# Numerators and seven-product sums accumulated in PSUM, the division on VectorE, and one more chunk in seven products

## The chip, the cores and the metric

The kernel runs on one core of a Trainium2 chip. A core has a matrix engine (TensorE, "PE" in the profile; its weight loads are "PEld"), three engines for elementwise work (VectorE "DVE", ScalarE "ACT", GpSimd "POOL") and a sync engine "SP", which here only issues DMAs. Each engine runs its own instructions strictly in the order of its own queue. Matmuls write into PSUM, eight banks of 2 KB per partition; DVE and ACT read and write PSUM and SBUF, in this kernel POOL touches SBUF only.

The metric is the device time of one execution in microseconds (us). Durations inside the execution come from one profiled execution.

## The reference

Two parts, one behind the other. First an attention with exponential features, for 8 batches and 8 heads, 576 positions of 64; then a feed-forward with the maximum of three projections, on 4608 tokens of 512:

```python
def phi(x):                                   # x: [8, 8, 576, 64], w_phi: [64, 128]
    proj = x @ w_phi
    proj = proj - max(abs(proj), axis=-1)
    return concat([exp(proj), exp(-proj)], axis=-1)
q_p, k_p = phi(q), phi(k)
kv  = einsum('bhsf,bhsd->bhfd', k_p, v);  z = sum(k_p, axis=2)
num = einsum('bhsf,bhfd->bhsd', q_p, kv)
den = einsum('bhsf,bhf->bhs', q_p, z)[..., None] + 1e-06
x = (num / den).transpose(0, 2, 1, 3).reshape(4608, 512)

h = maximum(maximum(x @ w1, x @ w2), x @ w3)  # w1, w2, w3: [512, 768]
out = h @ w_out                               # w_out: [768, 512]
```

## The kernel before

**Attention in 16 units.** A unit u is half a batch: four heads, that is two pairs `pr` of two heads `ab`. Per unit, PE projects keys and queries (line 545), DVE takes the maximum of the absolute values (line 549), and ACT takes the two exponentials `Ek` (line 553) and `Eq` (line 633) out of PSUM, for g = 0 and g = 1 (plus and minus). POOL multiplies the values with the exponentials of the key maxima (`vab`, line 597), PE makes the key-value matrices (`kvps`, line 616), which ACT or DVE copies to `kv_sb` (line 623).

**Numerators** (lines 674 to 743). For each of the four heads of a unit, PE makes ten products of 65 columns (64 of the numerator, 1 of the denominator): five blocks c of 128 positions for each g, into two banks `psn[0]` and `psn[1]` (line 683). DVE scales the first bank by `sq` into an SBUF tile `y` (line 692) and adds the second bank (line 695). For a pair of heads DVE then takes the reciprocal of the ten denominators (line 740) and POOL multiplies, `x_sb = y * rden` (line 741). From `x_sb` the tokens are turned into `xT`, by PE for units 0 and 1, by a DMA transpose on SP's queue for the others (line 773).

**Feed-forward in 9 chunks.** Chunk c (0 to 7) takes the first 512 positions of batch c, that is of units 2c and 2c+1; chunk 8 takes the last 64 positions of all batches. The weights are changed on the chip: w2 and w3 become w2 - w1 and w3 - w1 (six POOL subtractions, line 982), w1 @ w_out is made once (`pm`, line 1018), and h @ w_out becomes x @ (w1 @ w_out) (called straight, line 924) plus max(0, x(w2-w1), x(w3-w1)) @ w_out (called down, line 929). An ordinary chunk makes 12 groups of four 512-column matmuls (`ups`, line 891); the first six groups are relu'd out of PSUM by ACT or DVE (lines 905, 907), DVE takes the maximum with the other six (line 901).

**Chunks in seven products** (`seven_products`, lines 780 to 867; chunks 6, 7, 8). Here the two projections of a chunk are made as a 2 x 2 block product with seven products p1 to p7 in place of eight, of 256 columns (line 820), with sums of token blocks `sums` (four additions, `xs`, line 799) and sums of weight blocks `w_sums` (twelve POOL subtractions, `ws`, line 996). Every product has a bank of its own. For each of the three pairs of column blocks ACT copies p1 (line 845) and DVE makes seven additions (line 829), two of them for intermediate sums that stay in SBUF (u2, u3) and one (v) that is needed for one result; then two relus on ACT (line 862) and two maxima on DVE (line 864).

**What sets the order.** Every step is a node with a number, in the order in which the program creates it. A table written out by hand into the file (`PLAN`, read by `plan`, line 245) lists all nodes in the order in which they are emitted, with the engine that does each (T is PE, D DVE, A ACT, G POOL, S SP) and the indices of the buffers that it is the first to use, banks among them. So the table sets the order of every queue, the choice of engine where a step may go to several, and the sharing of the buffers. `fill` (line 268) puts idle matmuls between the early ones. The four weight loads are issued on POOL's queue (line 952); in the old table POOL issues w1, w_out and w2 right behind the loads of the first four units and w3 later.

## Time and profile before

| | |
|---|---|
| Time before, median of 3 runs | 276.3 us (275.75 to 281.68) |
| The profiled execution: its own time | 276.54 us |
| Its span, first to last instruction | 274.7 us |
| Mean granted clock of TensorE | 0.993 |
| PE, DVE, ACT, POOL busy | 265.6, 241.5, 214.2, 186.9 us |
| Chain of work that ended last, by engine | PE 89%, DVE 4%, ACT 3%, DMA 2% |
| `ups` of ordinary chunks, line 891 | 288 matmuls |
| `ups` of seven products, line 820 | 252 matmuls |
| DVE additions on seven products, line 829 | 63, 679 and 680 ns in the middle |
| POOL `x_sb`, line 741 | 32, 39.7 us |

A row of a group of instructions gives the line, the engine, the operation, what it writes and reads, the shapes and the count; then the busy time, the mean length of one, and the idle time ahead of it with what ended it. A row of windows gives a stretch of the span, and for each engine its busy time and the count in brackets. A row of the timeline or of the chain gives the start, the length and what ran. PE's ends are modelled: rows of neighbouring matmuls overlap, so PE's cost is read from the chain, where a group of n matmuls stands with the time that it took.

### The profile page before, as it was taken

The page shows a single profiled execution, that of the slowest core. Times are in us where ns is not written, and L with a number is a line of the kernel's source. Part 1 is how long each engine was busy: PE and PEld are TensorE (multiplying, and loading weights), DVE is VectorE, ACT ScalarE, POOL GpSimd, SP SyncE. Part 2 cuts the span into 40 slices and gives each one's busy share as a digit, 9 for nine tenths or more (in the row PEclk, how much of TensorE's full clock was granted, in tenths as well). Part 3 has the DMA queues.
Part 4 walks back from the last instruction along what each step waited for, and adds up shares of the span by engine and source line. Part 5 has one row for each costly group of instructions (what it writes and reads, how often), then busy time and mean ns, then how long its engine had stood idle before and what let it go on. Part 6 is the DMA issues. An engine that isn't in the chain of part 4 may idle for free.

```text
span 274.7 us, 8748 instructions
## 1 busy us (share of the span) xinstructions
PE 265.6 (97%) x3540; PEld 159.8 (58%) x3540; DVE 241.5 (88%) x489; ACT 214.2 (78%) x516; POOL 186.9 (68%) x183
## 2 busy tenths in 40 slices
PE   7789999999999999999999999999999999999994
PEld 4458744566565556565655455655548766686652
DVE  3799999999999888988888998999898999998871
ACT  3999999999999999779878989799987443254241
POOL 6798999999769951987569279937899856600000
PEclk9989999999999999999999999999999999999999
DMA  6999999999999999999999994596505053020253
GB/s 143 258 220 209 210 195 242 249 175 193 193 195 160 262 178 254 212 217 204 180 201 164 240 216 70 108 248 156 128 6 161 2 98 115 0 76 4 47 154 144
DMA packets 76200, 44.54 MB, mean 162 GB/s; under 512 B 52672, under 2 KB 67328, under 8 KB 76160
## 3 DMA queue, kind: packets, MB, share of 16 engines
q1 hardware_dynamic: 60880, 31.93, 53.6%
q0 software_dynamic: 14912, 11.77, 29.1%
q8 instruction: 27, 0.44, 0.6%
q10 hardware_dynamic: 368, 0.30, 0.3%
q14 instruction: 13, 0.11, 0.1%
HBM read 34.64 MB, written 9.44 MB: 160 GB/s over the span
## 4 chain that ended last, share of the span: by engine, by line
PE 89%; DVE 4%; ACT 3%; DMA 2%; issue 0%; POOLq 0%
PE ups L891 21%; PE ops L929 17%; PE ops L924 12%; PE ups L820 10%; PE psn L683 8%; PE kvps L616 7%; PE psm L642 3%; PE psq L545 3%; PE psk L545 3%; DMA qk_bf<-in_k_dram 2%; PE pm L1018 2%; ACT Eq L633 2%; DVE mk L549 2%; PE tps L508 1%; ACT Ek L553 1%; PE pst L545 1%
## 5 line engine op out<-in xcount | busy, mean ns | idle before, releaser
L633 ACT ACTIVATE Eq<-psm 128x512 bf16<-128x512 f32 (+1 forms) x160 | 81.7, 579 | 6.7 <-PE psm L642 6.1
L597 POOL TENSOR_TENSOR vab<-v_raw,em 128x1152 bf16<-128x1152 f32 (+1 forms) x36 | 68.3, 1906 | 17.5 <-ACT em L591 17.4
L553 ACT ACTIVATE Ek<-psk 128x512 bf16<-128x512 f32 x128 | 71.6, 641 | 2.2 <-DVE mk L549 1.2
L891 PE MATMUL ups<-xT,w_bf 128*128 128x512 bf16 x288 | 69.7, 380 | 0.0
L741 POOL TENSOR_TENSOR x_sb<-y,rden 128x640 bf16<-128x640 f32 x32 | 39.7, 1252 | 20.8 <-DVE rden L740 20.1
L929 PE MATMUL ops<-wout_bf,hT 128*128 128x512 bf16 (+2 forms) x222 | 52.0, 374 | 0.0
L549 DVE TENSOR_REDUCE mq<-psq 128x4 f32<-128x512 f32 x64 | 41.2, 681 | 4.8 <-PE psq L545 4.6
L549 DVE TENSOR_REDUCE mk<-psk 128x4 f32<-128x512 f32 x64 | 42.2, 681 | 2.2 <-PE psk L545 1.4
L891 PEld LDWEIGHTS <-w_bf 128*128 128x128 bf16 x288 | 25.0, 98 | 26.3 <-issue 1.3
L692 DVE TENSOR_TENSOR y<-psn,sq 128x325 f32<-128x325 f32 x64 | 30.6, 492 | 3.9 <-PE psn L683 3.1
L929 PEld LDWEIGHTS <-hT 128*128 128x128 bf16 x222 | 20.7, 98 | 21.7 <-DVE hT L864 0.5
L683 PEld LDWEIGHTS <-Eq 128*128 128x128 bf16 x640 | 26.1, 98 | 11.4 <-issue 2.3
L695 DVE TENSOR_TENSOR y<-y,psn 128x325 f32<-128x325 f32 x64 | 30.2, 487 | 2.1
L939 ACT COPY osb<-ops 128x512 f32<-128x512 f32 (+2 forms) x29 | 16.9, 582 | 17.2 <-PE ops L929 16.8
L829 DVE TENSOR_TENSOR parts<-ups,parts 128x512 f32<-128x512 f32 (+1 forms) x45 | 29.1, 679 | 1.1 <-PE ups L820 0.8
L683 PE MATMUL psn<-kv_sb,Eq 128*128 128x65 bf16 x640 | 28.7, 194 | 0.4 <-ACT Ek L553 0.4
L545 PEld LDWEIGHTS <-qkT 64*128 64x128 bf16 x576 | 18.6, 95 | 16.2 <-issue 12.3
L901 DVE TENSOR_TENSOR hT<-hT,ups 128x512 bf16<-128x512 bf16 x36 | 23.9, 676 | 2.0 <-PE ups L891 1.3
L924 PE MATMUL ops<-xT 128*128 128x512 bf16 x96 | 24.6, 381 | 0.0
L862 ACT ACTIVATE hT<-hT 128x512 bf16<-128x512 bf16 x18 | 10.8, 628 | 16.5 <-DVE hT L829 16.5
L616 PE MATMUL kvps<-vab,Ek 64*128 64x65 bf16 x1152 | 22.0, 192 | 0.0
L616 PEld LDWEIGHTS <-Ek 64*128 64x128 bf16 x1152 | 20.5, 96 | 1.0 <-issue 0.2
(84 smaller groups left out, 391.5 us busy)
## 6 DMA issues: line engine op xcount, KB each, us to landing
v_raw<-in_v_dram SPq DMA_DIRECT2D x16, 576.0 KB, 5.4
out_dram<-osb SPq DMA_DIRECT2D x31, 256.0 KB, 3.0
qk_bf<-in_k_dram POOLq DMA_DIRECT2D x15, 288.0 KB, 6.9
qk_bf<-in_q_dram POOLq DMA_DIRECT2D x15, 256.0 KB, 7.3
w_bf<-in_moe_w_dram POOLq DMA_DIRECT2D x3, 768.0 KB, 15.7
tail_raw<-in_q_dram SPq DMA_DIRECT2D x16, 64.0 KB, 4.6
out_dram<-osb SPq DMA_DIRECT2D x8, 128.0 KB, 2.3
wout_bf<-in_moe_w_out_dram POOLq DMA_DIRECT2D x1, 768.0 KB, 18.7
```

The source lines that it names most:

```text
L545: nc.tensor.matmul(ps[s]()[:, i, :], lhsT=qkT()[r, n, :], rhs=wph[r, :], start=True, stop=True)
L549: return nd(kind, {"DVE": 0.598 if n == 4 else 0.331}, lambda: nc.vector.tensor_reduce(dst(m()), ps()[:, 0:n, :], AXX, ALU.max, apply_abso ...
L553: return nd("ek", {"ACT": 0.478 if n == 4 else 0.264}, lambda: nc.scalar.activation(dst(Ek[g]()), ps()[:, 0:n, :], EXP, scale=1.0 - 2.0 * ...
L597: made.append(chosen(n_, lambda n_, g=g, t0=t0, t1=t1: (nc.vector if n_.eng == "DVE" else nc.gpsimd).tensor_tensor(vab()[:, g, t0:t1, 0:D] ...
L616: nc.tensor.matmul(kvps[ab]()[:, pr, g, :], lhsT=Ek[g]()[r, t, :], rhs=vab()[r, g, t, :], start=(pr == prs[0] and g + j == 0), stop=(pr == ...
L633: return nd("eq", {"ACT": 0.478 if n == 4 else 0.264}, lambda: nc.scalar.activation(Eq[g]()[:, t0:t0 + n, :], ps()[:, 0:n, :], EXP, scale= ...
L683: nc.tensor.matmul(psn[g]()[:, i, :], lhsT=Eq[g]()[:, t, :], rhs=kv()[:, pr, ab, g, :], start=True, stop=True)
L692: n_ = nd("xu", {"DVE": 0.064 + 0.0676 * n_t}, lambda: nc.vector.tensor_tensor(yv(y()), ps(0), sq_of(sq()).unsqueeze(len(shape) - 1).to_br ...
L741: divs[pr] = nd("x", {"POOL": 1.2}, lambda pr=pr, y=y, rden=rden: nc.gpsimd.tensor_tensor(x_sb()[:, pr].rearrange("p t a d -> p a t d"), y ...
L891: nc.tensor.matmul(ups()[:, o * n:(o + 1) * n], lhsT=w_bf[i + (not plain)][:, ct, jj * P:(jj + 1) * P], rhs=tokens_of(ct)[:, cols] if halv ...
L924: nc.tensor.matmul(ops_()[:, 0:hi - lo], lhsT=tile_of(ct, tt), rhs=line_w[c_i > MOVE][:, ct, lo:hi], start=(ct == 0), stop=False)
L929: nc.tensor.matmul(ops_()[:, 0:hi - lo], lhsT=hT()[:, j, tt * P:(tt + 1) * P], rhs=wout_bf[:, j, lo:hi], start=plain and j == 0, stop=(j = ...
```

## The change

Five things, all at once.

1. **Numerators in PSUM.** For each head, PE makes the five products of g = 0 into one bank; DVE scales that bank in place by `sq` (`xu`, PSUM to PSUM); PE then makes the five products of g = 1 onto the same bank, accumulating; DVE takes the reciprocal of five denominators out of PSUM (`xr`) and multiplies from PSUM into `x_sb` (`x`). The tile `y` and the second bank are gone. The multiplication is no longer on POOL.
2. **Seven-product sums in PSUM.** p6, p7 and p4 are accumulated onto p1's bank and p3 onto p5's. ACT or DVE copies the running sums to SBUF three times per pair (`kept`: s1, u2, u3), DVE makes three additions (c11, c22, c12), one operation that takes the maximum of the bank, zero and h (`hp`), and one maximum (`hx`) after one relu on ACT (`hr`).
3. **Chunk 5 in seven products too**, next to 6, 7 and 8.
4. **Sums of weights.** Three of the four live in an SBUF tile of their own, `w_sum`; the fourth overwrites half of w3 - w1 in place, after the last ordinary chunk has read it (chunk 4's last six groups). They no longer take buffers from the q and k loads.
5. **A new table** of 1752 nodes in place of 1687. `rden` gets eight buffers (it had three), the output tile `osb` three in place of four. Among the many moves of order: POOL issues w1 behind the first loads, w_out behind the first of the unit-0 products `vab`, and w2 and w3 only behind all `vab` products of units 0 and 1, w2 ahead of the key load of unit 4 and w3 behind it. w3's and w2's subtractions come after that, then `vab` of units 2 and 3.

```diff
-YS = 3
+YS = 8
-OSB = 4
+OSB = 3
-SEVEN = (6, 7, 8)
+SEVEN = (5, 6, 7, 8)
...
-            for pr in range(2):
-                y = buf("y", YS, [P, 2, 5, W], FP32)
-                rden = buf("rden", YS, [P, 2, 5, 1], FP32)
-                sums = [numerators(5, [(pr, ab, range(5))], lambda t, pr=pr, ab=ab: t[:, 2 * pr + ab, :],
-                                   (n_kvs[pr] + eqs[pr] + eqs["t"], [n_sq]), (y, lambda t, ab=ab: t[:, ab])) for ab in range(2)]
-                n_ = nd("xr", {"DVE": 0.122}, lambda y=y, rden=rden: nc.vector.reciprocal(rden(), y()[:, :, :, D:W]), sums, [y, rden])
-                divs[pr] = nd("x", {"POOL": 1.2}, lambda pr=pr, y=y, rden=rden: nc.gpsimd.tensor_tensor(
-                    x_sb()[:, pr].rearrange("p t a d -> p a t d"), y()[:, :, :, 0:D], rden().to_broadcast([P, 2, 5, D]), ALU.mult),
-                              [n_], [y, rden, x_sb], port=True)
+        def numerators(pr, ab, n_sq):
+            psn = bank("psn", [P, 5, W])
+            rden = buf("rden", YS, [P, 5, 1], FP32)
+
+            def nmm(g):
+                for c in range(5):
+                    t = 8 * (c % 2) + block(2 * pr + ab, c // 2) if c < 4 else NQ + pr
+                    nc.tensor.matmul(psn()[:, c, :], lhsT=Eq[g]()[:, t, :], rhs=kv()[:, pr, ab, g, :],
+                                     start=g + c == 0, stop=True,
+                                     skip_group_check=True)
+            ready = n_kvs[pr] + eqs[pr] + eqs["t"]
+            a = nd("N", {"PE": 0.157}, lambda: nmm(0), ready, [Eq[0], kv, psn])
+            n_ = nd("xu", {"DVE": 0.41}, lambda: nc.vector.tensor_tensor(
+                psn(), psn(), sq()[:, 2 * pr + ab, :].unsqueeze(2).to_broadcast([P, 5, W]), ALU.mult), [a, n_sq], [psn, sq],
+                    locks=[psn])
+            a = nd("N", {"PE": 0.157}, lambda: nmm(1), ready + [n_], [Eq[1], kv, psn])
+            n_ = nd("xr", {"DVE": 0.1}, lambda: nc.vector.reciprocal(rden(), psn()[:, :, D:W]), [a], [psn, rden], locks=[psn])
+            return nd("x", {"DVE": 0.4}, lambda: nc.vector.tensor_tensor(
+                x_sb()[:, pr, :, ab, :], psn()[:, :, 0:D], rden().to_broadcast([P, 5, D]), ALU.mult), [n_], [psn, rden, x_sb],
+                      locks=[psn])
...
-            p1 = product((0, 0), lambda: w_bf[1][:, 0:2], ready + d2, [])
-            s1 = chosen(ff("us", {"ACT": 0.482, "DVE": 0.598}, None, [p1[1]], [p1[0], one_], locks=[p1[0]]),
-                        lambda n_: copy_on[n_.eng](one()[:, 0], p1[0]()))
-            s1 = part(one, 0), one_, s1
-            p2 = product((0, 1), lambda: w_bf[1][:, 2:4], ready + d2, [])
-            own += [h(0), h(1)]
-            c11 = joined(p2, s1, own[0], hT)
-            p6 = product(1, lambda: w_sums[1](), [made[1], n_w[1][jp]], [sums_, w_tiles[1]])
-            u2 = part(one, 1), one_, joined(p6, s1, part(one, 1), one_)
-            p7 = product(2, lambda: w_sums[2](), [made[2], n_w[2][jp]], [sums_, w_tiles[2]])
-            u3 = part(two, 0), two_, joined(p7, u2, part(two, 0), two_)
-            p5 = product(0, lambda: w_sums[0](), [made[0], n_w[0][jp]], [sums_, w_tiles[0]])
-            c22 = joined(p5, u3, low(1), one_, [c11, u2[2]])
-            v_ = part(two, 1), two_, joined(p5, u2, part(two, 1), two_)
-            p4 = product((1, 1), lambda: w_sums[3](), [n_w[3][jp]], [w_tiles[3]])
-            c21 = joined(p4, u3, own[1], hT)
-            p3 = product(3, lambda: w_bf[2][:, 2:4], [made[3]] + d3, [sums_])
-            c12 = joined(p3, v_, low(0), one_, [c11, u2[2]])
...
+            p1 = product((0, 0), lambda: w_bf[1][:, 0:2], ready + d2, [])
+            chain = p1[0]
+            s1 = kept(p1, 0)
+            c11 = joined(product((0, 1), lambda: w_bf[1][:, 2:4], ready + d2, []), 0, h(0), [s1], hT)
+            p6 = product(1, lambda: w_sums[1](), [s1, made[1], n_w[1][jp]], [sums_], chain)
+            u2 = kept(p6, 1)
+            p7 = product(2, lambda: w_sums[2](), [u2, made[2], n_w[2][jp]], [sums_], chain)
+            u3 = kept(p7, 0, [c11])
+            p5 = product(0, lambda: w_sums[0](), [made[0], n_w[0][jp]], [sums_])
+            c22 = joined(p5, 0, h(1), [u3], hT)
+            p4 = product((1, 1), lambda: w_sums[3](), [u3, n_w[3][jp]], [], chain)
+            second.append(ff("hp", {"DVE": 0.598}, lambda: nc.vector.scalar_tensor_tensor(
+                h(1)(), runs(chain()), 0.0, h(1)(), ALU.max, ALU.max), [p4[1], c22], [chain, hT], locks=[chain]))
+            p3 = product(3, lambda: w_bf[2][:, 2:4], [c22, made[3]] + d3, [sums_], p5[0])
+            c12 = joined(p3, 1, lambda: runs(low()), [u2, c22], part_)
+            r_ = ff("hr", {"ACT": 0.478}, lambda: nc.scalar.activation(h(0)(), h(0)(), RELU), [c11], [hT])
+            first.append(ff("hx", {"DVE": 0.35}, lambda: nc.vector.tensor_tensor(h(0)(), h(0)(), runs(low()), ALU.max),
+                            [r_, c12], [part_, hT], port=True))
...
+                    if i == 1 and SEVEN:
+                        n_w[0][j // 2].deps.append(a)
...
-    w_tiles = [buf("w_sums", QK, [P, (1 + (BY_BATCH < UNITS)) * 2 * NB, D], BF16, of="qk_bf") for _ in range(4)]
-    w_sums = [lambda t=t: t()[:, 0:24, :].rearrange("p (c h) d -> p c (h d)", c=2) for t in w_tiles]
+    w_sum = const.tile([P, 3, 2, DFF], BF16, name="w_sum")
+    w_sums = [lambda: w_bf[2][:, 0:2]] + [lambda k=k: w_sum[:, k] for k in range(3)]
```

More of the change, by code (lines that the diff above doesn't have):

```diff
@@ L805, in pair, with whole, low, product @@
             js = (2 * jp, 2 * jp + 1)
-            one_, two_ = (buf("parts", RAW, [P, UT, D], FP32, of="raw") for _ in range(2))
-            def parts_of(t):
-                return lambda: t()[:, 0:16, :].rearrange("p (a o h) d -> p a o (h d)", a=2, o=2)
-            one, two = parts_of(one_), parts_of(two_)
+            part_ = buf("parts", RAW, [P, UT, D], FP32, of="raw")
             d2, d3 = diffs[0][jp], diffs[1][jp]
-            def product(moving, weight, deps, uses):
-                ps = bank("ups", [P, 2, n])
+            def whole(i):
+                return part_()[:, 8 * i:8 * i + 8, :].rearrange("p (o h) d -> p o (h d)", o=2)
+            def low():
+                return whole(0)[:, 0, :].bitcast(BF16).rearrange("p (o t) -> p o t", o=2)
+            def product(moving, weight, deps, uses, ps=None):
+                first_ = ps is None
+                ps = ps or bank("ups", [P, 2, n])
                 def fn():
```

417 lines of the change are left out of this document (182 added, 235 removed).

## Prediction

> **What bounds the kernel now.** I read the chain of waits first, then the busy time in stretches, then the groups of instructions. The page's first and fourth parts:
>
> ```profile
> span 274.7 us, 8748 instructions
> PE 265.6 (97%) x3540; PEld 159.8 (58%) x3540; DVE 241.5 (88%) x489; ACT 214.2 (78%) x516; POOL 186.9 (68%) x183
> ...
> PE 89%; DVE 4%; ACT 3%; DMA 2%; issue 0%; POOLq 0%
> ```
>
> The chain lies on PE for 89% of 274.7 us, about 244 us; the other 30 us are mostly the start and the last store. So what counts is PE's own work and whatever holds it up. In stretches (start:end and length, then busy time and count of PE, PEld, DVE, ACT, POOL; clock, DMA share, GB/s):
>
> ```profile
> 0.00:10.00 10.00, 7.02 (x66) 4.61 (x67) 3.96 (x8) 5.31 (x10) 6.59 (x16) 1.00 0.89 163
> 10.00:60.00 50.00, 48.05 (x781) 29.81 (x780) 49.04 (x104) 49.08 (x132) 46.95 (x46) 0.97 1.18 222
> 60.00:208.20 148.20, 148.20 (x2147) 83.02 (x2147) 132.37 (x272) 133.81 (x327) 110.52 (x99) 1.00 0.98 180
> 208.20:250.00 41.80, 41.69 (x429) 30.09 (x422) 41.22 (x81) 18.39 (x39) 22.83 (x25) 1.00 0.22 66
> 250.00:274.70 24.70, 20.69 (x133) 12.31 (x131) 14.94 (x28) 7.65 (x14) 0.00 (x0) 0.99 0.33 96
> ```
>
> 208.2 is where DVE ends the last query maximum of the attention. From 60 to 208 PE has no idle time and DVE rests 15.8 of 148.2 us, 10.7%. From 10 to 60 DVE and ACT are full (49.0 and 49.1 of 50), and from 208 to 250 DVE is full again (41.2 of 41.8) beside a full PE. POOL is never the fullest outside the start. So I cost PE first, then ask whether DVE can carry what is put on it by 208.
>
> **Part by part: PE.** The chain gives PE's real cost, since neighbouring rows overlap (start, length, what, count):
>
> ```profile
> 82.98 2.59 PE ups L891 x12
> 105.49 1.15 PE kvps L616 x72
> 134.27 0.62 PE psn L683 x20
> 240.29 4.37 PE ups L820 x40
> ```
>
> A 512-column `ups` takes 2.59/12 = 0.216 us, a 256-column product 4.37/40 = 0.109 us. Chunk 5 drops 48 of the first (10.4 us) and gets 84 of the second (9.2 us): 1.2 us less. The numerators stay at ten of 0.031 us per head: 0. Everything else on PE stays. PE's own gain is 1.2 us.
>
> **New waits on PE.** Per head, the second five numerators now stand behind DVE's scaling of the first five; per pair of a seven-product chunk, p6, p7 and p4 each stand behind a copy by ACT or DVE of the bank onto which they add, and p3 behind c22. What is queued behind a waiting product on PE is everything, as the queue is in order, and the maxima and exponentials of later units wait for that. The scaling takes 0.49 us and a copy 0.59 us (rows below); the cover is what the table puts between: another head's five (0.16 us), an `ups` group (0.86 us), the products of another pair. With no cover at all it would be 64 x 0.49 = 31 us and 36 x 0.59 = 21 us. PE waited for these engines before too, for banks and for `kv_sb`, so I take 0 where DVE keeps up; where it does not, it is the first rival.
>
> **DVE and ACT.** The groups, with busy time and mean ns:
>
> ```profile
> L741 POOL TENSOR_TENSOR x_sb<-y,rden 128x640 bf16<-128x640 f32 x32 | 39.7, 1252 | 20.8 <-DVE rden L740 20.1 <-POOL vab L597 0.6
> L692 DVE TENSOR_TENSOR y<-psn,sq 128x325 f32<-128x325 f32 x64 | 30.6, 492 | 3.9 <-PE psn L683 3.1 <-POOL x_sb L741 0.4
> L695 DVE TENSOR_TENSOR y<-y,psn 128x325 f32<-128x325 f32 x64 | 30.2, 487 | 2.1
> L901 DVE TENSOR_TENSOR hT<-hT,ups 128x512 bf16<-128x512 bf16 x36 | 23.9, 676 | 2.0 <-PE ups L891 1.3 <-ACT Eq L633 0.4
> L829 DVE TENSOR_TENSOR parts<-ups,parts 128x512 f32<-128x512 f32 x27 | 18.1, 681 | 1.1 <-PE ups L820 0.8
> L864 DVE TENSOR_TENSOR hT<-hT,parts 128x512 bf16<-128x512 bf16 x18 | 8.4, 492 | 0.2
> L740 DVE RECIPROCAL rden<-y 128x10 f32<-128x10 f32 x32 | 6.5, 207 | 0.1
> L623 DVE CAST kv_sb<-kvps 128x260 bf16<-128x260 f32 x13 | 5.3, 422 | 1.3 <-PE kvps L616 1.0
> L845 ACT COPY parts<-ups 128x512 f32<-128x512 f32 x9 | 5.1, 587 | 6.8 <-DVE hT L829 3.8 <-PE ups L820 1.4 <-DVE hT L864 0.8
> ```
>
> Neighbours on DVE overlap:
>
> ```profile
> 24.04 0.90 DVE L692 TENSOR_TENSOR y<-psn,sq 128x325 f32<-128x325 f32 x2 [0.30 <-PE psn L683]
> 236.13 2.47 DVE L829 TENSOR_TENSOR parts<-ups,parts 128x512 f32<-128x512 f32 x4
> ```
>
> Two of 0.49 take 0.90, four of 0.68 take 2.47: 0.08 us each is shared. Net of that I use 0.41 for 325 columns, 0.60 for 512, 0.13 for a reciprocal, 0.41 for a maximum in SBUF, 0.34 for a `kv_sb` copy.
>
> No row shows DVE writing PSUM, nor a reciprocal or a product with broadcast out of PSUM. For the scaling the nearest row is L692, the same read with SBUF as target; for the multiplication L695, which reads PSUM and 325 columns against 320. Both have 0.49, and I take it; the ends are 0.42 (the `kv_sb` copy out of PSUM) and 0.68 (the 512-wide row). The reciprocal of five is put at L740's price. `hp` is put at L901's. Over the whole run the reciprocals double (32 to 64), the multiplications replace the additions one for one, the seven-product part loses 27 of its 63 additions and 6 of 18 maxima, and gets 12 `hp` and 6 copies: DVE's total hardly moves. But it moves in time. The tail gets lighter, the stretch before 208.2 heavier.
>
> The two tables, counted in DVE's order up to the last query maximum of unit 15, hold 382 instructions before (as the windows do) and 432 after. The difference: reciprocals +28; nine additions, three `hp` and three copies of seven products (one copy is chunk 6's) +15; their maxima in SBUF +3; chunk 5's ordinary maxima -6; relus put on DVE +3; `kv_sb` copies +5; others +2. In time: 28 x 0.13 + 15 x 0.60 + 3 x 0.41 - 6 x 0.60 + 3 x 0.60 + 5 x 0.34 + about 0.9 = 14.7 us, as much as the 15.8 us that DVE rested from 60 to 208. PE's order moves too: ahead of the last `kvps` the new table has one straight and one down of chunk 5 more (ten matmuls of 0.216 us) and a first product of chunk 6 (0.4), less the 1.2 us saved: 1.4 us more PE work ahead of that point and 2.6 less behind it. So PE alone would reach the point at 208.2 + 1.4 = 209.6. DVE, with all 14.7 us put behind 60, needs 132.4 + 14.7 = 147.1 us; resting 1.4 to 1.9%, as it does in its full stretches, it gets there at 209.2 to 210.0. The two fall together, and I take PE's: DVE costs nothing on top. ACT has five instructions fewer up to the end of unit 15, some 3 us at the 0.59 us of L845: nothing.
>
> [...]
>
> **POOL and the start.** 32 multiplications of 1.25 us go. In the start POOL looks like the path, with the weights' subtractions behind four of them and `vab` behind those:
>
> ```profile
> 15.02 1.16 POOL L597 TENSOR_TENSOR vab<-v_raw,em 128x576 bf16<-128x576 f32 x1
> ...
> 32.17 2.48 POOL L741 TENSOR_TENSOR x_sb<-y,rden 128x640 bf16<-128x640 f32 x2
> 34.62 12.53 POOL L982 TENSOR_TENSOR w_bf<-w_bf 128x1024 bf16<-128x1024 bf16 x6
> 47.12 6.26 POOL L597 TENSOR_TENSOR vab<-v_raw,em 128x1152 bf16<-128x1152 f32 x3
> ```
>
> That promises 4 x 1.25 = 5 us. But the subtractions need w2, then w3. The issues of w2, of unit 4's keys behind it, and of w3, each with its time to landing:
>
> ```profile
> L952 POOL DMA_DIRECT2D w_bf<-in_moe_w_dram x1: 802/802/802, 12.1 to 12.1; - x1
> DMA to landing us min/median/max: 21.6/21.6/21.6
> ...
> L442 POOL DMA_DIRECT2D qk_bf<-in_k_dram x1: 701/701/701, 14.2 to 14.2; - x1
> DMA to landing us min/median/max: 21.1/21.1/21.1
> ...
> L952 POOL DMA_DIRECT2D w_bf<-in_moe_w_dram x1: 803/803/803, 24.5 to 24.5; - x1
> DMA to landing us min/median/max: 14.5/14.5/14.5
> ```
>
> w2 landed at 33.7, the keys at 35.3, w3 at 39.0, whatever their issue: POOL's DMA queue drains in order, with DMA full (share 1.18 from 10 to 60). The new table issues w2 only behind eight `vab` of 1.16 us and the issue of w_out, at about 25 us, but w2, keys, w3 keep their order. If the queue has not run dry by then, they land as before, the subtractions begin at 33.7 in place of 34.6, and the gain is 0.9 us at most, of which I take 0, as DVE and ACT are full there. If it runs dry, that is the second rival.
>
> **The rest at nothing.** SP's transposes (line 773) wait for DVE in place of POOL, and behind them on SP stand stores and loads; a chunk starts some 30 us after its x. The in-place weight sum puts 6 POOL steps of 1.15 us between chunk 4's last `ups` and chunk 5's p5 and p6; POOL rests 37.7 us in that stretch, and if the cover goes, it costs up to 1.2 us a pair. Three `osb` in place of four: stores are 2 to 3 us apart and land in 3.
>
> **Sum.** 276.5 - 1.2 = 275.3 for an execution like the profiled one, which stood 0.24 us above the median of 276.3: 275.1, and with a few tenths for new waits that the cover misses, 275.3. 2% is 5.5 us, about what a measurement of this kernel tells from no change.
>
> **Rivals.** *DVE becomes the bound of the middle.* Place: 60 to 208; price: the 15 us above. It decides where DVE cannot go below its rest. At a rest of s the point comes at 60 + 147.1/(1-s), and the end is 276.5 plus what that is beyond 208.2, less 2.6: 2% gives 275.8, 5% 280.5, 10.7% as now 290. It is slower by 2% from a rest of 6% on. For it: DVE's new work is a chain PE, DVE, PE, DVE, DVE on one bank, with waits both ways. Against: DVE does run at 1.4% rest beside a full PE in 208 to 250. If each of the 168 numerator operations ahead of the point cost 0.05 us more than taken, that is 8.4 us more, and at 2% of rest 284. [...] Chance of DVE bound 0.30, of it 0.13 beyond 2%.
>
> *w2 and w3 come late.* If w2, issued at 25, takes the 14.5 us that w3 took, it lands at 39.7 and the subtractions start 5.1 us late: 280.4. Against: the landing times above fit a full queue. 0.10, of it 0.03 beyond 2%.
>
> *The start tightens.* From 47 to 56 the chain runs over ACT, its 3% or 8 us in all:
>
> ```profile
> 50.22 2.53 ACT Eq L633 x6
> 53.41 2.53 ACT Ek L553 x6
> ```
>
> If the new order, with fewer exits on ACT and no multiplication on POOL, keeps PE supplied there, half of it gives 276.5 - 1.2 - 4 = 271.3, all of it 267.3. For it: 8 us are there to be had. Against: ACT's exponentials stay, 49 of 50 us full, and DVE gets more. 0.17, of it 0.11 beyond 2%.
>
> *The forecast's own case:* the accumulation does not do for the time what it does for the counts, since POOL and the tail's DVE were not the path, and chunk 5's 1.2 us is left. 0.43, 272.5 to 278.
>
> **Numbers.** Faster by over 2%: 0.11. Slower: 0.13 + 0.03 = 0.16. Within: 0.73. The range 271 to 282.5 leaves out about a tenth on each side.
>
> **What would show it.** Right: DVE at 97 to 99% from 60 to 208 and PE still without idle time; the last query maximum at 209 to 211; the end some 60 us behind it; DVE well under full after 215; w2 landing at 33 to 35; `xu` and `x` at 0.48 to 0.50, `xr` at 0.2. Wrong: PE idle on DVE at the second numerators (first rival), POOL idle ahead of the weights' subtractions (second), a chain that no longer passes over ACT between 40 and 60 (third).

## The result, and the profile after

| | before | after |
|---|---|---|
| Median | 276.21 us (4 executions, 275.75 to 281.68) | 278.29 us (4 executions, 277.93 to 278.63) |
| Ratio, 95% interval | | 1.0081 (1.0060 to 1.0101) |
| Profiled execution, its span | 276.54, 274.7 us | 278.21, 276.1 us |

The 281.68 of before is a disturbed execution and does not enter the ratio. The change costs 0.8%, 2.1 us: within 2%, as the likeliest case had it, but on the other side of zero than the 1.2 us less that were forecast. By the profiled spans the loss is 1.4 us.

The first and fourth parts of the page of after:

```profile
span 276.1 us, 8805 instructions
...
PE 263.2 (95%) x3544; PEld 163.1 (59%) x3580; DVE 236.2 (86%) x512; ACT 214.9 (78%) x514; POOL 150.6 (55%) x154
...
PE 83%; ACT 4%; DMA 3%; POOL 3%; DVE 3%; issue 2%; POOLq 0%; DVEq 0%
```

The 263.2 us of PE can't be set against before's 265.6. This trace holds 3544 products for 3580 weight loads (before 3540 for 3540); the 36 missing ones are `ups` of ordinary chunks (14), straight (17), down (4) and `pm` (1), all but a few of 512 columns. A later run with the same products on PE in the same order (unit 5's queries early, below) has all 3580 recorded, and there PE is busy for 265.8 us. So PE is not busy for less time than before. The stretches of after, with the columns as in the prediction:

```profile
10.00:60.00 50.00, 46.33 (x684) 27.89 (x687) 46.48 (x107) 47.41 (x119) 42.18 (x41) 1.00 1.17 225
60.00:208.20 148.20, 145.48 (x2203) 86.65 (x2228) 137.22 (x306) 130.94 (x322) 84.94 (x81) 1.00 0.98 180
208.20:250.00 41.80, 41.59 (x472) 31.14 (x469) 35.54 (x71) 25.50 (x55) 17.81 (x19) 1.00 0.22 68
250.00:276.10 26.10, 21.97 (x132) 12.46 (x132) 12.46 (x22) 5.69 (x11) 0.00 (x0) 0.97 0.28 81
```

From 60 to 208 PE had no idle time and now has 2.7 of 148.2 us, while DVE rests 7.4% (10.7% before). The idle time is an upper bound, since the missing products leave gaps. So I also took the starts of PE's weight loads, which are all recorded, and for each the distance to the next less what that kind of product takes at its fastest quarter in six kernels. In this ledger, an estimate, PE's waits behind 30 us grow by 1.8 us (3.8 to 5.6). They grow by 1.8 from 60 to 82 us (0.5 to 2.3), shrink by 0.2 ahead of that and grow by 0.2 behind it. Another 0.6 us is in the usual distances between the kinds of products, which the order of PE decides. With the 1.2 us of work that the prediction counted as saved, and 0.2 lost in the first 30 us, that is the 1.4 us of the spans. Only the growth from 60 to 82 us is clearly larger than what such a ledger leaves open; the other parts are of that size. The stretch where the waits are, first of before, then of after:

```profile
62.00:75.00 13.00, 13.00 (x221) 7.66 (x218) 12.45 (x29) 12.70 (x31) 10.63 (x10) 1.00 1.13 189
```

```profile
62.00:75.00 13.00, 11.63 (x275) 7.77 (x271) 12.09 (x29) 13.00 (x32) 11.85 (x12) 1.00 1.13 191
```

PE rests 1.4 us there, and ACT has become full. But before was nearly as full in this stretch (DVE 12.45, ACT 12.70 of 13.00 us, the DMA share 1.13) and PE had no idle time, so full engines alone don't make PE wait. The table of PE's waits in after from 62 to 75 us (who waited, for whom, us, times, longest):

```profile
PE psk L551 <- issue: 0.6, 1, 0.6
...
PE kvps L622 <- ACT osb L895: 0.3, 1, 0.3
PE ops L880 <- ACT Eq L639: 0.3, 1, 0.3
...
PE kvps L622 <- ACT kv_sb L629: 0.2, 1, 0.2
```

Together 1.3 us in four waits; before's table has none of PE for that stretch. The three shorter ones, 0.7 us together, are for banks that ACT had to read first. The longest is not: PE stops from 74.33 to 74.90 us, between the sixth and the last two of eight `psk` products, with no semaphore to wait for ("issue"). What stopped it stays open. The same stop stands in three of the variants below (0.9 us without `xu`, 0.6 and 0.5 with ACT relieved), and not in four others (two places, POOL, both with unit 5's queries early), which were no faster. The chain of after, from 61 to 73 us (start, length, what):

```profile
60.71 1.30 PE kvps L622 x72
62.01 0.36 ACT kv_sb L629
62.38 0.50 ACT Ek L559
62.88 0.27 ACT kv_sb L629
63.14 2.03 ACT Ek L559 x5
65.18 0.48 ACT osb L895
65.66 1.00 ACT Eq L639 x2
...
66.70 0.38 PE ops L880
...
67.13 0.59 PE ops L880 x2
...
67.73 0.11 ACT em L597
67.83 1.95 ACT Ek L559 x4
69.78 0.48 ACT osb L895
70.26 1.48 ACT Eq L639 x3
71.74 0.23 ACT vab L607
71.97 0.22 ACT kv_sb L629
...
72.22 1.33 PE kvps L622 x72
```

The chain lies on ACT for 9.1 us here. Before, it lay on ACT for 8.8 us from 47 to 56 and not at all in this stretch. Read by the chain, the new order has moved ACT's tight place some 15 us down rather than removed it. That this is what PE pays for is argued, not shown: only 0.7 us of its waits here are for ACT.

### The profile page after: what moved, and what is told of

Same layout as the page of the kernel before. It is cut to its first block, busy times and chain, and to the rows that moved or that the text cites. A ratio compares the mean times of both kernels' runs of the same rounds, so it can differ in the third digit from the quotient of the medians.

```text
span 276.1 us, 8805 instructions
## 1 busy us (share of the span) xinstructions
PE 263.2 (95%) x3544; PEld 163.1 (59%) x3580; DVE 236.2 (86%) x512; ACT 214.9 (78%) x514; POOL 150.6 (55%) x154
## 4 chain that ended last, share of the span: by engine, by line
PE 83%; ACT 4%; DMA 3%; POOL 3%; DVE 3%; issue 2%; POOLq 0%; DVEq 0%
PE ups L845 19%; PE ops L885 15%; PE ups L780 13%; PE ops L880 10%; PE psn L686 7%; PE kvps L622 6%; DMA qk_bf<-in_q_dram 3%; PE psm L648 3%; PE psq L551 3%; PE psk L551 2%; ACT Ek L559 2%; PE pm L973 2%; POOL vab L603 2%; DVE mq L555 1%; PE pst L551 1%
## 5 line engine op out<-in xcount | busy, mean ns | idle before, releaser
L639 ACT ACTIVATE Eq<-psm 128x512 bf16<-128x512 f32 (+1 forms) x160 | 80.0, 592 | 6.4 <-PE psm L648 4.6
L845 PE MATMUL ups<-xT,w_bf 128*128 128x512 bf16 x226 | 57.8, 379 | 0.7
L686 PEld LDWEIGHTS <-Eq 128*128 128x128 bf16 x640 | 28.5, 98 | 12.6 <-issue 1.3
L845 PEld LDWEIGHTS <-w_bf 128*128 128x128 bf16 x240 | 20.6, 98 | 21.0 <-issue 1.4
L691 DVE TENSOR_TENSOR psn<-psn,sq 128x325 f32<-128x325 f32 x64 | 30.2, 495 | 3.2 <-PE psn L686 2.5
L686 PE MATMUL psn<-kv_sb,Eq 128*128 128x65 bf16 x640 | 32.3, 194 | 0.2 <-DVE psn L691 0.2
L696 DVE TENSOR_TENSOR x_sb<-psn,rden 128x320 bf16<-128x320 f32 x64 | 28.9, 478 | 0.4
L788 ACT COPY parts<-ups 128x512 f32<-128x512 f32 x30 | 17.3, 600 | 8.9 <-PE ups L780 5.4
L855 DVE TENSOR_TENSOR hT<-hT,ups 128x512 bf16<-128x512 bf16 x30 | 20.2, 682 | 1.7 <-PE ups L845 1.1
L798 DVE TENSOR_TENSOR hT<-ups,parts 128x512 bf16<-128x512 f32 x24 | 16.1, 683 | 5.5 <-PE ups L780 3.9
L780 PEld LDWEIGHTS <-w_bf 128*128 128x128 bf16 x192 | 18.0, 98 | 4.0 <-DVE x_sb L696 0.2
```

Of the source, the lines that this page charges most:

```text
L639: return nd("eq", {"ACT": 0.478 if n == 4 else 0.264}, lambda: nc.scalar.activation(Eq[g]()[:, t0:t0 + n, :], ps()[:, 0:n, :], EXP, scale= ...
L686: nc.tensor.matmul(psn()[:, c, :], lhsT=Eq[g]()[:, t, :], rhs=kv()[:, pr, ab, g, :], start=g + c == 0, stop=True, skip_group_check=True)
L691: n_ = nd("xu", {"DVE": 0.41}, lambda: nc.vector.tensor_tensor(psn(), psn(), sq()[:, 2 * pr + ab, :].unsqueeze(2).to_broadcast([P, 5, W]), ...
L780: nc.tensor.matmul(ps()[:, o, :].rearrange("p (b t) -> p b t", t=m.shape[-1]) if len(m.shape) == 4 else ps()[:, o, :], lhsT=weight()[:, c, ...
L845: nc.tensor.matmul(ups()[:, o * n:(o + 1) * n], lhsT=w_bf[i + (not plain)][:, ct, jj * P:(jj + 1) * P], rhs=tokens_of(ct)[:, cols] if halv ...
```

## The experiments

**One part at a time.** Two kernels are the old kernel with one part of the change: the numerators (part 1 of the list above), or the seven-product sums for chunks 6 to 8 (part 2), in an order as near to the old table as the part allows. The third is the changed kernel with chunk 5 as ordinary groups, which is one word and a table without chunk 5's new nodes, otherwise in the new order:

```diff
-SEVEN = (5, 6, 7, 8)
+SEVEN = (6, 7, 8)
```

> The kernel before with the new numerators alone: one bank, xu in place, second five, xr, x on DVE, in the order of before, into which only these nodes are put; seven-product chunks and weight sums as before. Numerators theory (the split numerators cost PE its waits for xu, spread over 62 to 213 us): 277.5 to 279, most of the 2.1 us that the whole change lost. Order theory (the parts cost nothing, the new table's order makes late units K at 62 to 75 and 198 to 207 us): 276.2 within 0.7. Chunk 5 theory: 276.2 within 0.7 as well. If POOL's relief were worth something by itself: under 275.5.

> The kernel before with the new seven-product sums alone for chunks 6, 7 and 8 (p6, p7 and p4 accumulated onto p1 in one bank with copies between them, p3 onto p5, hp), weight sums still in the slots of the q and k tiles, order of before with only these nodes put in. It lies behind 208 us. All three theories: 276.2 within 0.7, since the lag of PE did not grow behind 215 us in the changed kernel. If the copies stand in PE's way: up to 3 x 3 x 0.6 us = 5.4 us, 281.

> The changed kernel with chunk 5 as twelve ordinary groups again (48 matmuls of 512 columns in place of 84 of 256), its order otherwise that of the new table; the weight sums wait for chunk 5 as the code asks. Chunk 5 theory (its copies, its sums and the early weight sums make ACT and POOL late at 180 to 213 us): 276 to 277, the loss gone. Numerators theory and order theory: PE's nominal 1.2 us come back, 279 to 279.7; if the seven products save nothing on PE: 278.3.

Measured: numerators alone 281.28 us, ratio 1.0186 (1.0151 to 1.0221); sums alone 277.23, 1.0043 (1.0013 to 1.0074); the changed kernel without chunk 5's seven products 280.27, 1.0158 (1.0116 to 1.0200). Undoing chunk 5 costs 2.0 us (280.27 less 278.29), and the two intervals are apart. The other two parts lose, the numerators far more than the sums. But none of these three has an order that was made for it, and the next runs show what that can be worth.

**Other orders of the same instructions.** Here the instructions and what they compute stay; only their places in the table change, for example (its first words, before and after the search)

```diff
-3A@0.7 1D@0.8 4A@1.3 6A@3.7 107G0@1.2 10S0@0.7 0G@1.9 5D@3.7 11D1@4.0 12A@4.0 19T0@4.5 20D0@5.0 29T12@5.5
+3A@0.3 13S0@0.3 1D@0.3 107G0@0.5 10S@0.7 2D@0.5 9G1@1.2 11D@3.8 4A@0.7 106G@2.0 12A@3.8 0G@2.8 7D@4.2 5D@4.4
```

The first two have before's engines and another placing of the numerators, without and with the new sums; the next four are the changed kernel in three orders and once with 61 instructions on another engine; the last is the old kernel in a new order.

> The kernel before with the new numerators alone, as in the first run of them, but with the new nodes put in so that their place respects two things that the first run's trace showed: the two readers of a PSUM bank on DVE and ACT take turns in the order written, and a bf16 maximum on DVE stands still while POOL works on SBUF (1.36 us in place of 0.42). Order theory: most of the 4.7 us that the first of them lost was the place of the nodes, so 276.2 to 277.9. Numerators theory (the part itself costs, wherever its nodes stand): 279.5 to 281.5. A third theory, DVE load at the end: x of the last two units comes to DVE behind 208 us, where the old seven products still have 63 sums on DVE; then 277.5 to 278.5 here, and the loss lies behind 208 us.

> The kernel before with the new numerators and the new seven-product sums of chunks 6, 7 and 8 (chunk 5 ordinary, weight sums in the slots of q and k), order of before with the new nodes put in as in the run beside it. Order theory: the parts cost nothing, 276.2 within 0.7. Numerators theory: 279.5 to 281.5 as without the sums. Load at the end: the new sums take DVE work off the end, so 276 to 277, under the run with the numerators alone by 1 us or more.

> The changed kernel, every instruction as it is and on its engine, with another order within each engine's stream and other buffer numbers (an order searched on a model of the queues that was set by the two traces). Order theory: the loss is the order's, so 276 or less; with the 1.2 us of chunk 5, 275. Numerators theory: the waits for xu are a property of the part and stay, 277.5 to 278.5. Chunk 5 theory: 277.5 to 278.5.

> The changed kernel, every instruction on its engine, everything planned before 32 us as in the new table, behind that another order within the streams of PE, DVE, ACT and POOL (DMA issues keep their order), searched with a model of the queues that has the readers' turns and the stop of DVE under POOL. Order theory: the 2.1 us come back and chunk 5's 1.2 us with them, 274.5 to 276. Numerators or chunk 5 theory (a property of the parts): 277.5 to 278.5.

> As the run beside it, and some 65 copies may change between ACT and DVE or POOL as well (t1, kv, osb, copies of sums, the differences of x quarters), nothing else. Order theory: 273.5 to 275.5, below the run with the order alone. If the balance of the engines, not the order, is what lacks: this one gains over 1 us on the run with the order alone. Numerators or chunk 5 theory: 277.5 to 278.5.

> The changed kernel once more in an order of its own behind 32 us, every instruction on its engine; the order is searched anew with a slack that the last runs showed to be needed: the second five of a numerator that follow their xu within 0.15 us hold PE for 0.41 us in place of 0.22. Order theory: 274.5 to 277, so the table and not the parts lost the 2.1 us. If the new parts lose whatever the order: 278 to 280 again. If it is as far off as the other two searched orders (289 and 293): what the order must respect is still not known, and the theory stays open.

> Control: the kernel before, every instruction on its engine, everything before 32 us as it is, behind that in an order searched in the same way as for the changed kernel. By the model of the queues both searched orders come out alike (269.6 for the old parts, 269.8 for the new). If the new parts are worth nothing once each has its order: this run and the other lie within 1 us of each other. If the parts gain PE's 1.2 us: the other is 1 to 2 us below this one. Old numerators have no tight pairs, so a searched order should hurt them less: 275 to 279.

| kernel | median, us | ratio to before (95%) |
|---|---|---|
| numerators, other placing | 284.75 | 1.0303 (1.0277 to 1.0328) |
| numerators and sums, other placing | 282.07 | 1.0223 (1.0193 to 1.0252) |
| changed, every place searched anew | 310.33 | 1.1227 (1.1172 to 1.1283) |
| changed, new order behind 32 us | 289.18 | 1.0453 (1.0408 to 1.0497) |
| the same and 61 engines changed | 293.17 | 1.0583 (1.0549 to 1.0617) |
| changed, new order with slack | 284.42 | 1.0324 (1.0301 to 1.0346) |
| old kernel, new order with slack | 279.52 | 1.0153 (1.0117 to 1.0190) |

Numerators and sums together have no other run to compare with. The other six are slower than the kernel whose instructions they share, by 3 to 32 us (the one with 61 engines changed by 15). The whole change is worth 2 us, so an order can count for more than the parts, and the 5 us of the numerators alone say little about numerators. That some order makes the changed kernel faster is not shown: none was found. The worst one shows what an order can spoil. Its longest waits of PE, then of ACT:

```profile
PE ups L836 <- DMA xT<-x_sb: 6.8, 2, 4.9
PE tps L505 <- DMA qk_bf<-in_q_dram: 3.7, 1, 3.7
```

```profile
ACT Ek L550 <- DVE mk L546: 18.1, 21, 4.1
```

ACT's exponentials waited 18 us for the maxima that DVE takes out of the same bank, though neither needs the other's result. In this program the two readers of a bank go in the order in which they are written: the later one waits for a semaphore of the earlier.

**Do the new waits on DVE cost anything?** The changed kernel with `xu` left out: the scaling by `sq` isn't done, and the second five numerators wait for nothing but the bank.

```diff
-            n_ = nd("xu", {"DVE": 0.41}, lambda: nc.vector.tensor_tensor(
-                psn(), psn(), sq()[:, 2 * pr + ab, :].unsqueeze(2).to_broadcast([P, 5, W]), ALU.mult), [a, n_sq], [psn, sq],
-                    locks=[psn])
+            n_ = nd("xu", {"DVE": 0.41}, lambda: None, [a, n_sq], [psn, sq], locks=[psn])
```

> The changed kernel with its table, without the product xu (the first half of a numerator isn't scaled by the exponent of the query's maximum): DVE has 64 x 0.40 = 26 us less to do, and the second five follow the first five without a wait. Order theory: PE's own work is unchanged, the few numerators whose second five followed xu closely give back 10 x 0.19 = 1.9 us at most: 276.4 to 278.3. Numerators theory (waits for xu and DVE behind them make the loss): 274.5 to 276, back to before's time with chunk 5's 1.2 us on top.

Measured 278.67 us, ratio 1.0101 (1.0082 to 1.0120): no change. Its page has DVE at 212.4 us in place of 236.2:

```profile
PE 263.8 (95%) x3544; PEld 163.5 (59%) x3580; DVE 212.4 (77%) x448; ACT 215.0 (78%) x514; POOL 150.5 (54%) x154
```

Taking 24 us of work from DVE and 64 waits from PE gains nothing. Behind 82 us neither DVE's load nor the second numerators' wait is the cause, as the starts of the products show to the hundredth (below). Ahead of it the run shows no gain, but it has waits of its own there: 0.9 us for transposed queries and 0.9 us of "issue".

**The two places where PE waits.** A ledger of waits pointed to 54 to 84 and to 180 to 214 us. Only there the order was changed.

> The changed kernel with its table, in which only what starts at 54 to 84 us and at 180 to 214 us is put in another order within PE, DVE, ACT and POOL (at the second place POOL's copies of the last tokens of chunks 9 and 11 go ahead of vab of unit 14, at the first place C of unit 6 and the weight sums go ahead of vab of units 3 to 5); DMA issues and engines as they are. Two places theory (the loss sits where PE fell behind, at 62 to 75 and 196 to 213): 276 to 277. If these places only show a loss that comes from elsewhere: 278 within 0.7.

Measured 277.91 us, 1.0084 (1.0069 to 1.0098), against 278.29 and 1.0081: the same. The starts of the same products (below) say why: the second place got 1.0 us shorter, the first 0.8 longer.

**ACT's load and POOL's load.** Key exponentials that take four blocks take one, in two units, and the key matrices read computed blocks twice, so these kernels leave work out; for POOL, half of the `vab` products of units 3 to 5 is left out and the other half read twice.

```diff
+            some = 1 if n == 4 and u in (3, 4) else n
-                dst(Ek[g]()), ps()[:, 0:n, :], EXP, scale=1.0 - 2.0 * g), [a, n_tab], [ps, Ek[g]], locks=[ps])
+                dst(Ek[g]())[:, 0:some], ps()[:, 0:some, :], EXP, scale=1.0 - 2.0 * g), [a, n_tab], [ps, Ek[g]], locks=[ps])
...
+                t2 = PT if u in (3, 4, 5) else t1
-                made.append(chosen(n_, lambda n_, g=g, t0=t0, t1=t1: (nc.vector if n_.eng == "DVE" else nc.gpsimd).tensor_tensor(
+                made.append(chosen(n_, lambda n_, g=g, t0=t0, t1=t2: (nc.vector if n_.eng == "DVE" else nc.gpsimd).tensor_tensor(
```

> The changed kernel with its table; the exponentials of the keys of units 3 and 4 are computed for one block of four only (16 of the 0.48 us kind become about 0.16: 5 us of ACT less between 33 and 62 us), and K of these units reads the computed blocks twice in place of the others, so that it has as many matmuls. Front theory (up to 75 us ACT is what PE waits for; ACT rested 3.5 us after 10 us there in place of 0.9, and PE is 1.4 us late at 75): 276.3 to 277.2. Order spread over the whole kernel, or PE's own work: 278.3 within 0.4.

> The same taken from units 9 and 10, which run at 110 to 150 us: as many instructions, as many us of ACT. Front theory: nothing waits for ACT there, 278.3 within 0.4. If ACT bounds the middle too: 276 to 277.5.

> The same taken from units 3 and 4 of the kernel before. Front theory: before's PE hardly waits at 62 to 75, so 276.2 less 0 to 0.6. If ACT bounds the first 75 us of both kernels: 274.5 to 275.3, as large a gain as in the changed one, and then the changed kernel's loss isn't ACT's rests alone.

> The changed kernel with its table; vab of units 3, 4 and 5 is computed for the first of its two halves only (6 instructions of 2.1 us become 1.1: 6 us of POOL less between 54 and 72 us), and K reads that half twice. Rival to the front theory (K of unit 5 at 72.2 us comes right after vab at 72.0, so POOL is what PE waits for): 276.3 to 277.5. Front theory: 278.3 within 0.4.

Measured: ACT in units 3 and 4 278.49 us (1.0082, 1.0058 to 1.0107), in units 9 and 10 278.24 (1.0066, 1.0038 to 1.0094), in the old kernel's units 3 and 4 276.03 (0.9996, 0.9967 to 1.0025): no gain anywhere. The theory that ACT's load up to 62 us holds the kernel falls. But the same stretch in the run with units 3 and 4 shows that this run did not reach the tight place:

```profile
62.00:75.00 13.00, 11.63 (x275) 7.78 (x271) 12.07 (x29) 12.99 (x32) 11.86 (x12) 1.00 1.16 193
```

ACT is as full there as before, since what it does from 62 us on hangs on the key matrices that PE makes then, and these came when they came. POOL's relief did not help: 280.41 us (1.0129, 1.0071 to 1.0187), an interval that overlaps the changed kernel's, with executions from 277.9 to 281.8. The profiled one is the longest of them, and the longest wait of PE in it from 62 to 78 us is

```profile
PE ups L846 <- DMA xT<-x_sb: 2.8, 1, 2.8
```

**The tight place itself.** Two last kernels. The first moves one load and one transpose of unit 5's queries ahead (the words are 422G and 427S of the table, each taken from its old place; the lines are shortened); the second does that and shortens the key exponentials of unit 5, which lie in ACT's full stretch.

```diff
-184T3@28.3 1236G@35.7 181T@28.5
+184T3@28.3 1236G@35.7 422G@37.0 181T@28.5
...
-352S2@49.5 323T7@59.7
+352S2@49.5 427S@50.0 323T7@59.7
...
+            some = 1 if n == 4 and u == 5 else n
```

> The changed kernel with one load and one transpose moved, all engines' other work in its order: the load of the queries of unit 5 (issued at 52.8 us, landed at 59.7) goes ahead of POOL's later weight subtractions, to about 38 us, and its transpose on SP (issued at 63.4, landed at 69.4, behind the store of the first output rows) goes ahead of that store, to about 49 us. Nothing of the computation is left out. Theory 'a crowd of transposes': between 61 and 75 us four transposes stand on SP one behind the other, the last (x of unit 3, landed 74.5) only 0.6 us ahead of chunk 1's first product; with one of them gone the others land about 2 us sooner, and the 1.4 us for which PE rests in 62 to 75 go: 276.6 to 277.2 us. Theory 'ACT full': PE rests there because ACT has no idle time from 62 to 76 us and the chain lies on it for 9 us; an earlier transpose changes nothing: 278.0 to 278.5. Worse than 279 would be neither.

> As the kernel with unit 5's queries loaded and transposed early, and the eight key exponentials of unit 5 that take four blocks take one (they lie at 62 to 70 us, inside ACT's full stretch; the key matrices read computed blocks twice, so three of four exponentials of this unit are left out): about 2.9 us less of ACT in 62 to 75. Theory 'ACT full' with 'a crowd of transposes' as the next bound: PE's idle time in 62 to 75 falls from 1.4 to under 0.5 us and the end comes 0.9 to 1.5 us sooner than in the changed kernel: 276.7 to 277.4, whichever the other kernel of this call gives. Theory 'the loss has no place of its own' (what is saved in one stretch is waited for in the next, as when other units' exponentials were shortened): 278.0 to 278.6.

Measured: 278.87 us (1.0108, 1.0073 to 1.0143) and 278.69 us (1.0104, 1.0069 to 1.0138): none of the gain that the crowd of transposes, or ACT together with it, asked for. The second kernel's executions lie between 277.5 and 280.8; the profiled one is the shortest of them, and its span is 275.7, 0.4 under the changed kernel's. PE's waits from 62 to 77 us, of the first and of the second:

```profile
PE kvps L622 <- POOL vab L603: 1.1, 1, 1.1
PE kvps L622 <- ACT osb L895: 0.3, 1, 0.3
PE ops L880 <- ACT Eq L639: 0.3, 1, 0.3
PE kvps L622 <- ACT kv_sb L629: 0.2, 1, 0.2
```

```profile
PE kvps L623 <- POOL vab L604: 0.4, 1, 0.4
PE ops L881 <- ACT Eq L640: 0.3, 1, 0.3
```

The transposes were not it: with one moved away the three waits for ACT stand, and POOL's `vab` of unit 5 comes 1.1 us late. POOL had waited 1.7 us for its values, whose load now stands behind the moved transpose on SP. With ACT shortened too, two waits for ACT go, POOL's is the longest, and PE rests 0.75 us from 62 to 75, more than the 0.5 that was asked for. The starts of the same five products in the changed kernel and in its variants, from the traces, in us:

```
                                    changed  no xu  ACT 3,4  ACT 9,10  POOL 3-5  q5     q5+ACT  two places
kvps of unit 4                        69.83  70.32    69.84     69.88     69.81   69.90   69.66    70.19
kvps of unit 5                        72.19  72.32    72.20     72.23     71.94   72.25   71.82    72.95
chunk 1, first product on unit 3's x  75.06  75.57    75.07     75.02     74.08   75.69   74.52    76.11
a numerator of unit 4                 81.88  82.39    81.89     81.84     85.31   82.52   81.34    82.69
a product of chunk 7                 265.38 265.89   265.39    265.34    268.94  266.71  264.94   265.22
last less the one above it           183.50 183.50   183.50    183.50    183.63  184.19  183.60   182.53
```

Two things are to be read. What a kernel gains or loses by 82 us it nearly keeps to the end. And from there on PE takes 183.5 us in four of them to the hundredth, with 24 us of DVE or 5 us of ACT taken away: behind 82 us the time is PE's own order. The changed kernel's table of waits has none of PE from 80 to 270 us. The exception is the kernel with unit 5's queries early, which loses 0.7 us more by 103 us; PE waits 0.5 us there for ACT's copy of an output tile.

## Why the prediction was wrong

**Chunk 5: the sign right.** Its seven products were put at 1.2 us less on PE; undoing them costs 2.0 us. How much of that is the order of the kernel without them is not known, and PE's busy time does not show the saving (265.8 us where all products are recorded, 265.6 before).

**PE's waits: this step failed.** The prediction said that PE waited for banks and for `kv_sb` before too, took "0 where DVE keeps up", and put 0.2 into its sum, "a few tenths for new waits that the cover misses". DVE kept up (leaving `xu` out gains nothing), and by the ledger PE's waits grew by 1.8 us all the same, between 60 and 82 us; an estimated 0.6 more went into PE's order, for which the sum has no term. That outweighs the 1.2 us that was counted as saved, so the time went up and not down. And the waits that grew are not the new ones that were weighed: none from 62 to 75 us is for `xu` or for a copy of a seven-product chunk. They are of the old kinds, moved by the new order. That the time still fell within 2% is luck in part: the saving that was to be left over did not show in PE's busy time, and the loss was small.

Why PE waits there is open in part. The products of key matrices of unit 5 could start when four things were done, and these came at 71.97 (ACT's cast for `vab`), 72.00 (POOL's `vab`), 72.07 (DVE's `kv_sb`) and 72.19 us (ACT's `kv_sb`); chunk 1's first product on unit 3's tokens, at 75.06, had its bank at 74.24 and its transposed tokens at 74.47, and stood behind the unexplained stop up to 74.90. So every relief of one engine showed another: a wait of 2.8 us for transposed tokens after POOL's (in the longest execution), `vab` 1.1 us late after the load's, 0.5 us gained at 75 us after ACT's (in the shortest). No single wait can be named whose removal gives the time back. That ACT's full stretch is a part of it is supported by the last run's trace, but not by its median; a kernel that relieves ACT, POOL and the transposes together was not tried, nor one without the stop alone.

**DVE (first rival): did not come.** Its work did move ahead, by about as many instructions as counted: up to the last query maximum the windows hold 436 (12, 107 and 317 up to 215.0 us) where 432 were counted, and 384 before, not 382. But DVE is 92.6% busy from 60 to 208, not 97 to 99%, and the run without `xu` shows that it has room to spare. It waited for PE ahead of `xu` for 0.8 us in that stretch (2.5 in the whole run, row of L691 below). The last query maximum ends at 215.0, not 209 to 211:

```profile
214.31 0.68 DVE L555 TENSOR_REDUCE mq<-psq 128x4 f32<-128x512 f32 x1
```

The estimate took PE alone to reach that point at 209.6. PE's last query products start at 212.5 us (206.5 before), 6 us later. The counts up to there explain 2.4 of it, not the 1.4 forecast: one unit's 72 products of key matrices more (1.2 us) stand ahead of them in the new order, since the prediction counted up to the last `kvps` and not to the last query product. The waits and the order above are the most of the rest.

**The prices: right.** The groups of after:

```profile
L691 DVE TENSOR_TENSOR psn<-psn,sq 128x325 f32<-128x325 f32 x64 | 30.2, 495 | 3.2 <-PE psn L686 2.5 <-ACT sq L667 0.4
L696 DVE TENSOR_TENSOR x_sb<-psn,rden 128x320 bf16<-128x320 f32 x64 | 28.9, 478 | 0.4
L695 DVE RECIPROCAL rden<-psn 128x5 f32<-128x5 f32 x64 | 10.3, 180 | 0.8 <-PE psn L686 0.4
L812 DVE SCALAR_TENSOR_TENSOR hT<-ups,hT 128x512 bf16<-128x512 f32 x12 | 8.2, 684 | 0.3 <-PE ups L780 0.2
```

0.48 to 0.50 for `xu` and `x` and 0.2 for `xr` were forecast. Writing PSUM cost DVE what writing SBUF did, 495 beside 492 ns. The reciprocal of five out of PSUM took 180 ns where that of ten out of SBUF took 207: reading PSUM did not make it longer than the price taken for it. The two differ in columns as well, so what the PSUM read alone costs they don't tell.

**Start and weights: as forecast, the second rival did not come.** The issues of w2 and w3 in after, and the subtractions:

```profile
24.28 0.82 POOL L908 DMA_DIRECT2D w_bf<-in_moe_w_dram  x1
...
26.02 0.77 POOL L908 DMA_DIRECT2D w_bf<-in_moe_w_dram  x1
...
33.12 10.44 POOL L938 TENSOR_TENSOR w_bf<-w_bf 128x1024 bf16<-128x1024 bf16 x5 [4.65 <-DMA w_bf<-in_moe_w_dram]
```

Issued at 24.3, w2 is there at 33.1 (33 to 35 forecast), and POOL rests 4.7 us for it. POOL idle ahead of the subtractions was named as the sign of this rival; it came although w2 was on time, so the sign did not tell the two cases apart. The subtractions begin 1.5 us sooner than before; what that is worth no run shows.

**Third rival: it came half true.** It promised up to 8 us if the chain left ACT between 47 and 56 us. The chain did: it lies on PE from 44 to 62 us. The gain did not come. ACT's work in all was not less (214.9 us, 214.2 before), and the chain has 9.1 us of ACT some 15 us later. So the ACT time on the chain was not time to be had here.

## What to carry to other kernels

In a kernel whose order is written out for every engine, a change of parts comes with a new order, and an order can weigh more than the parts (here 3 to 32 us, beside 2.1 for the whole change): cost old waits anew, stretch by stretch, and not only the ones that the change adds. Full engines alone don't tell where PE will wait: from 62 to 75 us both kernels were about as full (DVE 12.45 and 12.09, ACT 12.70 and 13.00 of 13.00 us), and one waited, for 1.4 us. Removing the wait that the profile names gave nothing back here, as another came in its place. To learn what an operation on another engine costs, leave it out and look at the starts of the same products: where they keep their distances, as the 183.50 us with and without `xu` behind 82 us, it costs nothing there.

## What the runs showed of the hardware

**Two readers of a PSUM bank took turns as written.** In the changed kernel with every place searched anew (310.33 us) ACT waited 18.1 us for DVE's maxima, on banks from which both read. The wait is for a semaphore in the program; what the bank would allow without it no run shows. A search that lets them overlap promises time that is not there in this program.

**Two maxima on DVE ended only after the POOL work beside them.** A maximum of two bf16 tiles in SBUF took 0.41 to 0.43 us in 16 of 18 cases in before. The two that start while a POOL product or sum of two SBUF tiles is running take 0.82 and 1.37 and end 0.28 us after it; one that runs beside a POOL copy takes 0.42. The durations of line 864 in before (min, median, max), then a pair of them on DVE and what POOL did:

```profile
L864 DVE TENSOR_TENSOR hT<-hT,parts x18: 408/418/1371, 223.3 to 266.3; 128x512 bf16<-128x512 bf16 x18
```

```profile
231.86 1.71 DVE L864 TENSOR_TENSOR hT<-hT,parts 128x512 bf16<-128x512 bf16 x2
```

```profile
232.02 1.26 POOL L799 TENSOR_TENSOR sums<-xT,sums 128x512 bf16<-128x512 bf16 x1 [1.39 <-DVE sums L799]
```

**A weight load ahead of a wait made a product look long.** The expectations of two runs say that the second five numerators, where they start within 0.15 us of the end of their `xu`, hold PE for 0.41 us in place of 0.22. Counted from the weight load it is 0.34 beside 0.16 us (medians) in the changed kernel, but four of the six loads that are that close started before `xu` ended. Counted from their first product's start to the next product's, the five take 0.15 to 0.16 us (median) whether they are that close (6 of 64 in the changed kernel, 24 of 64 in numerators and sums in their other placing) or not. So the difference is a wait for `xu`, not a slower product.
